# A second MLP in runs of four groups, and two pairs of attention steps of TensorE joined

## The chip, the cores and the metric

The kernel runs on one core of a Trainium2 chip. The metric is the device time of one execution in microseconds (us). The profile comes from one further execution, taken with the hardware profiler on. In what follows PE is TensorE (its matmuls; PEld are its weight loads, which have a row of their own), DVE is VectorE, ACT is ScalarE, POOL is GpSimd and SP is SyncE.

## The reference

```python
for t in range(S):                       # attention with a decaying state, 4 x 8 heads, S = 768, D = 48
    cur = einsum('bhd,bhe->bhde', u * kt, vt)
    y[:, :, t] = einsum('bhd,bhde->bhe', rt, state + cur)
    state = wt * state + einsum('bhd,bhe->bhde', kt, vt)
x = y as (3072 tokens, 384)
x = ((x @ w_a) * (x @ w_b)) @ w_out      # first MLP, 1536 hidden
h = x @ w_in                             # second MLP, 2048 hidden
out = (max(h, 0) + alpha * min(h, 0)) @ w_out2
```

All inputs and the output are float32.

## The kernel before

The sequence is cut into 12 units of the attention, two to a block of 512 tokens; six blocks (`BLOCKS`) go through the first MLP (`mlp1`), and after it six chunks of 512 tokens go through the second (`mlp2`). The attention of the next block is computed beside the first MLP of this one; the second MLP stands alone behind them.

Nothing is issued in the order of the text. Each step is a task (`add`): an engine, a planned duration, a priority (lower goes first), a function that emits the instructions, the names that it reads and writes, and at most one buffer that it takes (`alloc`). `Tasks.run` simulates the engines with the planned durations, picks on each engine the ready task of the lowest priority, and so makes one fixed order for each engine. Buffers of one tag are handed out in the order in which the tasks were added, and a task whose buffer is not free is passed over. On the chip the engines then follow that order, and wait on each other by semaphores; a planned duration alters the order and nothing else.

A product of the MLPs is split in high and low parts (fp32r): `gemm3` is nine matmuls 128*128 on 128x512, three over the depth times (high, high), (low, high), (high, low).

*Second MLP.* A chunk has 16 groups f of 128 hidden channels. `step(f)` computes `hp` (nine matmuls of 512 columns, `gh`, L769 through the helper `mm`) in one of two PSUM banks (tag "h"); DVE makes the leaky rectifier in two instructions (`neg` L923, `pos` L927) in a tile m (tag "a2", three buffers); ACT makes the high part g/h (`hi` L932) and DVE the low part g/l (`lo`, L257) in a tile of tag "g22" (three buffers). `add_out(f)` multiplies g by the output weights in twelve matmuls of 384 columns into four accumulators `acd` (`out2`); three are in banks of tag "acc", the fourth in one of tag "att". The list of tasks puts `add_out(f-1)` behind `step(f)` at the same priority, and which of the two goes first is left to the planner. The weights of both kinds, "i" and "p", are loaded alternately (`w2`) by POOL, and ACT and DVE turn them from float64 into two float32 parts during the last block of the first MLP.

*Attention.* A unit has a tree of decay products on T (DVE), levels `psl` (PE, L567) that read T, then `ktrans`, two steps of four transposes of k from T into two PSUM banks `psk` (PE, L613), each copied by ACT to `kn` (L618); `dstate` (`psd`, L637); `state`; and `yout`, two steps (halves b = 0, 1) of y^T, `psx` (PE, L710), each turned by ACT (L720) and DVE into the first MLP's x. The levels of most units, `psk`, `psd` and `psx` share three banks of tag "att". T has one buffer: the next unit's T is loaded when the last reader of this one is done, and `psk` is among the last.

Of the kernel before, what the change touches and what calls it, by code (L numbers as in the profile page):

```python
# [211 lines left out]
def rwkv_then_moe_kernel(  # L212
# [43 lines left out]
    def tt(out, a, b, op=ALU.mult):  # L256
        nc.vector.tensor_tensor(out=out, in0=a, in1=b, op=op)  # L257
# [4 lines left out]
    def act(n, psum=False):  # L262
        return n / 1200 + (0.05 if psum else 0.093)
# [72 lines left out]
    def unit(u, pr):  # L336
# [34 lines left out]
        def mn(hd, k):  # L371
            return f"M{hd}{k}" if u else f"m{hd}/{k}"

        def zn(cc, hd, k):
            return f"Z{cc}{hd}{k}" if u else f"z{cc}{hd}/{k}"
# [226 lines left out]
            else:  # L602
                nc.scalar.copy(dst, src)

        def ktrans(g, p):
            st = {}
            ps = f"psk{u}_{g}"
# [7 lines left out]
            def cp():  # L615
# [5 lines left out]
            add("ACT", act(448, True), p, cp, r=[ps], w=[f"{kn}/{g}"], alloc=("kn", kn) if g == 0 else None)  # L621

        def dstate(p):

# [67 lines left out]

                add("ACT", act(384, True), p + 6, begin, r=[f"psd{u}_{cc}"], w=s)

        def yout(b, p):


            st = {}
            ps = f"psx{u}_{b}"
            t0 = 256 * (u - us[0]) + 128 * b  # L700
            tag, pool = bank(False)

            def mms():
                st["ps"] = pp.tile([128, 3, 128], F32, tag=tag, name="psx", bufs=3)
                for cc in range(2):
                    for q in range(4):
                        for s, c0, hd, beg, end in (
                                (2 * q, 0, 0, True, True), (2 * q + 1, 32, 1, True, True),
                                (8 + q, 32, 0, True, False), (8 + q, 0, 1, False, True)):
                            nc.tensor.matmul(  # L710
                                out=st["ps"][32 * (s % 4):32 * (s % 4) + 32, s // 4, 64 * cc:64 * cc + 64],
                                lhsT=zt(cc, hd)[:, 4 * b + q, c0:c0 + 32],
                                rhs=mt(hd)[:, cc, 4 * b + q],
                                start=beg, stop=end,
                            )

            def hi():
                if first:
                    X[j] = xp.tile([128, 2, 3, 256 * len(us)], F32R, tag="x", name="x", bufs=2)
                nc.scalar.copy(X[j][:, 0, :, t0:t0 + 128], st["ps"])  # L720

            def lo():
                tt(X[j][:, 1, :, t0:t0 + 128], st["ps"], X[j][:, 0, :, t0:t0 + 128].bitcast(F32), ALU.subtract)

            first = u == us[0] and b == 0
# [3 lines left out]
            add("ACT", act(384, True), p, hi, r=[ps], w=[f"x{j}/{u}{b}h"], alloc=("x", f"x{j}") if first else None)  # L729
            add("DVE", dve(384), p, lo, r=[ps, f"x{j}/{u}{b}h"], w=[f"x{j}/{u}{b}l"])  # L730


        if u:
# [22 lines left out]
        for g in range(2):  # L756
            ktrans(g, pr(0.6))
# [4 lines left out]
        yout(0, pr(0.8))  # L762
        yout(1, pr(0.85))

        return [f"x{j}/{u}{b}{z}" for b in range(2) for z in "hl"]

# [97 lines left out]
    def load_x2(c, p):  # L864
# [20 lines left out]
            add("DVE", dve(512), p, lo, r=[s, f"{xn}/{kt}h"], w=[f"{xn}/{kt}l"])  # L885
        return [f"{xn}/{kt}{z}" for kt in range(3) for z in "hl"]

    def mlp2(c, pr, xn):
        acc = f"acc2_{c}"
        st = {"acc": {}}  # L890

        def out2(f, ks, ts=(0, 1, 2, 3)):
            if f == 0:
                st["acc"][ts[0]] = pp.tile(
                    [128, DM], F32, tag="acc" if ts[0] < 3 else "att", name=f"acd{ts[0]}", bufs=3)
            for i in ks:
                wi, gi = ((0, 0), (1, 0), (0, 1))[i]
                for t in ts:
                    mm(st["acc"][t], st["g", f][:, gi, 128 * t:128 * t + 128], W["p", f][:, wi],
                       f == 0 and i == 0, f == F2 - 1 and i == 2)  # L900

        def add_out(f, p):
            g, wo = f"h{c}_{f}", f"wp{f}"
            accs = [f"{acc}_{t}" for t in range(4)]
            if f in (0, F2 - 1):
                for t in range(4):
                    add("PE", 3 * 0.162, p, lambda t=t: out2(f, (0, 1, 2), (t,)),
                        r=[g + "/h", g + "/l", wo, wo + "/l"], w=[accs[t]],
                        alloc=("psacc" if t < 3 else "psatt", accs[t]) if f == 0 else None)
                return  # L910
            add("PE", 8 * 0.162, p, lambda: out2(f, (0, 1)), r=[g + "/h", wo, wo + "/l"], w=accs)
            add("PE", 4 * 0.162, p, lambda: out2(f, (2,)), r=[g + "/l", wo], w=accs)

        def step(f, p):
            h, m, g = f"ph{c}_{f}", f"m{c}_{f}", f"h{c}_{f}"

            def gh():
                st["h", f] = pp.tile([128, 512], F32, tag="h", name="hp", bufs=2)
                gemm3(st["h", f], W["i", f], X["2", c])

            def neg():
                st["m", f] = P2["p"].tile([128, 512], F32, tag="a2", name="g", bufs=3)
                nc.vector.tensor_scalar(  # L923
                    out=st["m", f], in0=st["h", f], scalar1=0.0, scalar2=al[:, f:f + 1], op0=ALU.min, op1=ALU.mult)

            def pos():
                nc.vector.scalar_tensor_tensor(  # L927
                    out=st["m", f], in0=st["h", f], scalar=0.0, in1=st["m", f], op0=ALU.max, op1=ALU.add)

            def hi():  # L930
                st["g", f] = P2["p"].tile([128, 2, 512], F32R, tag="g22", name="g22", bufs=3)
# [8 lines left out]
            add("ACT", act(512), p - 50, hi, r=[m], w=[g + "/h"], alloc=("g22", g))  # L940
            add("DVE", dve(512), p - 50, lo, r=[m, g + "/h"], w=[g + "/l"])

        for f in range(F2):
            step(f, pr(f))
            if f:
                add_out(f - 1, pr(f))
            elif c:
                st2[c - 1](pr(f))
        def last(p):
            add_out(F2 - 1, p)  # L950
            for t in range(4):
                o = f"o{c}_{t}"

                def cp(t=t):
                    st["o", t] = P2["p"].tile([128, DM], F32, tag="o", name="o", bufs=4)
                    if t % 2:
                        nc.vector.tensor_copy(st["o", t], st["acc"][t])
                    else:
                        nc.scalar.copy(st["o", t], st["acc"][t])

                def wr(t=t):
                    nc.sync.dma_start(out=out[t * S + c * CH:t * S + c * CH + CH, :], in_=st["o", t])

                add("DVE" if t % 2 else "ACT", dve(384) if t % 2 else act(384, True), p - 50, cp, r=[f"{acc}_{t}"], w=[o],
                    alloc=("o", o))
                add("SP", 0.6, p - 50, wr, r=[o], nbytes=128 * 1536)
        st2[c] = last
# [22 lines left out]
    with tc.manual_schedule():  # L990
# [155 lines left out]
```

## Time and profile before

| what | value |
|---|---|
| median of 3 runs | 1027.59 us (1027.45 to 1028.16) |
| profiled execution, its own time | 1034.63 us |
| span of that execution, first to last instruction | 1032.8 us |
| PE busy | 988.8 us (96%) |
| DVE busy | 728.4 us (71%) |
| ACT busy | 434.1 us (42%) |
| granted TensorE clock, mean over the span | 0.986 |

The profiled execution is 7.04 us longer than the median of the runs without a profile. A busy share is a mean over stages that have different limits. Matmuls are pipelined: a row's length holds the tail of its last matmul, so the time that a run of matmuls takes from PE is read from its start to the start of the next row. A row of the timeline merges neighbours of one kind, "x9" being nine matmuls.

### The profile page before, as it was taken

The numbers are of one execution on the slowest core, as the hardware profiler recorded it, in microseconds if no ns is written. First come the engines' busy times: TensorE is split into PE (matmuls) and PEld (weight loads), VectorE is DVE, ScalarE is ACT, GpSimd is POOL, SyncE is SP. The second block draws the span as 40 slices with busy tenths as digits, with TensorE's granted clock in tenths as the row PEclk, the third lists the DMA queues.
The fourth block names the chain that finished last, engine by engine and source line by source line (L and its number), as shares of the span: only waits on it lengthen the run. The fifth ranks groups of instructions, "written<-read, shape, count | busy, mean of one in ns | idle before, by whom it ended". The sixth has DMA issues, their size and how long they took to land.

```text
span 1032.8 us, 22660 instructions
## 1 busy us (share of the span) xinstructions
PE 988.8 (96%) x9616; PEld 850.3 (82%) x9616; DVE 728.4 (71%) x1215; ACT 434.1 (42%) x930; POOL 95.7 (9%) x173
## 2 busy tenths in 40 slices
PE   6869889999999999999999999999999999999998
PEld 5768767778788888878888887989998999999988
DVE  7868897989899898797944667455554554555544
ACT  2475989354353553534347995121221211221111
POOL 3032350100000010001003431000000000000000
PEclk9898999999999999999999999999999999999999
DMA  9483585051441424325115552010010100000000
GB/s 278 107 233 110 143 248 137 33 138 36 130 133 21 125 69 120 88 55 169 20 42 168 169 183 78 1 31 31 1 55 7 31 31 1 1 31 1 31 1 31
DMA packets 75092, 85.70 MB, mean 83 GB/s; under 512 B 55216, under 2 KB 64560, under 8 KB 72368
## 3 DMA queue, kind: packets, MB, share of 16 engines
q1 hardware_dynamic: 67824, 52.81, 19.2%
q0 software_dynamic: 7168, 31.46, 9.5%
q8 instruction: 75, 1.23, 0.5%
q14 instruction: 25, 0.20, 0.1%
HBM read 73.24 MB, written 11.01 MB: 82 GB/s over the span
## 4 chain that ended last, share of the span: by engine, by line
PE 65%; DVE 12%; ACT 10%; DMA 9%; issue 3%; SPq 1%; POOL 0%; ACTq 0%; DVEq 0%; POOLq 0%
PE acd L769 19%; PE hp L769 19%; PE acc L769 7%; PE pa L769 6%; PE pb L769 6%; DVE T L257 3%; DMA T<-in_rkw_t_dram 3%; DVE e L257 2%; PE psl L567 2%; DVE A L486 2%; PE warm L988 2%; ACT ws L301 2%; DMA n<-in_rkw_n_dram 2%; ACT ws L295 2%; PE psx L710 2%
## 5 line engine op out<-in xcount | busy, mean ns | idle before, releaser
L769 PE MATMUL acd<-w,g 128*128 128x384 f32 x1152 | 216.9, 336 | 0.2 <-ACT x L855 0.2
L769 PE MATMUL hp<-x,w 128*128 128x512 f32 x864 | 214.9, 393 | 1.5 <-DVE g L927 1.5
L769 PEld LDWEIGHTS acd<-w,g 128*128 128x128 f32 x1152 | 203.8, 188 | 8.6 <-ACT x L855 0.5
L932 ACT CAST g<-g 128x512 fp32r<-128x512 f32 x96 | 59.8, 623 | 304.1 <-PE acd L769 262.1
L769 PEld LDWEIGHTS hp<-x,w 128*128 128x128 f32 x864 | 161.1, 188 | 31.5 <-DVE g L927 1.9
L769 PE MATMUL acc<-g,w 128*128 128x512 f32 x648 | 173.9, 396 | 0.0
L257 DVE TENSOR_TENSOR g<-g,g 128x512 fp32r<-128x512 f32 x96 | 66.2, 690 | 150.6 <-ACT g L932 150.6
L769 PE MATMUL pb<-x,w 128*128 128x512 f32 x648 | 161.2, 393 | 1.7 <-issue 1.7
L769 PE MATMUL pa<-x,w 128*128 128x512 f32 x648 | 160.7, 392 | 0.0
L769 PEld LDWEIGHTS pb<-x,w 128*128 128x128 f32 x648 | 121.4, 189 | 27.7 <-issue 2.1
L769 PEld LDWEIGHTS pa<-x,w 128*128 128x128 f32 x648 | 120.7, 188 | 26.5 <-ACT w L316 0.5
L769 PEld LDWEIGHTS acc<-g,w 128*128 128x128 f32 x648 | 118.5, 188 | 24.1
L257 DVE TENSOR_TENSOR T<-T 112x1024 f32<-112x1024 f32 (+3 forms) x144 | 116.5, 811 | 21.2 <-DMA T<-in_rkw_t_dram 17.2
L831 ACT CAST g<-a 128x512 fp32r<-128x512 f32 x72 | 44.6, 620 | 132.6 <-DVE a L257 130.0
L923 DVE TENSOR_SCALAR g<-hp,al 128x512 f32<-128x512 f32 x96 | 72.1, 751 | 25.5 <-PE hp L769 23.0
L486 DVE TENSOR_REDUCE A<-e 128x16 f32<-128x768 f32 (+15 forms) x148 | 86.1, 582 | 1.7
L257 DVE TENSOR_TENSOR a<-a,pb 128x512 f32<-128x512 f32 x72 | 49.2, 683 | 28.1 <-PE pb L769 25.7
L927 DVE SCALAR_TENSOR_TENSOR g<-hp,g 128x512 f32<-128x512 f32 x96 | 66.3, 691 | 3.0
L820 ACT COPY a<-pa 128x512 f32<-128x512 f32 x72 | 42.1, 584 | 36.2 <-PE pa L769 35.8
L257 DVE TENSOR_TENSOR g<-a,g 128x512 fp32r<-128x512 f32 x72 | 49.6, 689 | 10.0 <-ACT g L831 10.0
L567 PEld LDWEIGHTS psl<-T 48*16 48x16 f32 (+3 forms) x3072 | 34.3, 99 | 25.8 <-issue 12.2
L567 PE MATMUL psl<-T 48*16 48x16 f32 (+3 forms) x3072 | 38.0, 183 | 15.2 <-DVE T L257 8.4
(68 smaller groups left out, 900.0 us busy)
## 6 DMA issues: line engine op xcount, KB each, us to landing
raw<-in_wt_dram POOLq DMA_DIRECT2D x68, 384.0 KB, 4.1
T<-in_rkw_t_dram SPq DMA_DIRECT2D x12, 1344.0 KB, 9.0
N<-in_rkw_n_dram SPq DMA_DIRECT2D x10, 1152.0 KB, 8.4
x2d<-x POOLq DMA_DIRECT2D x36, 128.0 KB, 2.1
x2r<-x2d SPq DMA_DIRECT2D x36, 128.0 KB, 2.3
out_dram<-o SPq DMA_DIRECT2D x24, 192.0 KB, 1.9
V<-in_v_s_dram SPq DMA_DIRECT2D x11, 384.0 KB, 8.5
Z<-in_v_s_dram SPq DMA_DIRECT2D x44, 96.0 KB, 3.1
```

Of the source, the lines that this page charges most:

```text
L257: nc.vector.tensor_tensor(out=out, in0=a, in1=b, op=op)
L295: nc.scalar.activation(out=c["s"].bitcast(F16).rearrange("p (n b) -> p n b", b=2)[:, :, 1], in_=c["raw"][:, :, 1].bitcast(F32), func=ACTF. ...
L301: nc.scalar.activation(out=c["s"].bitcast(U16).rearrange("p (n b) -> p n b", b=2)[:, :, 0], in_=c["raw"][:, :, 0], func=ACTF.Copy, scale=7 ...
L486: nc.vector.tensor_reduce(out=v[:, :, d:d + (n - 1) * (SUB + 1) + 1:SUB + 1], in_=part(st["e"], 0, n), axis=AX.X, op=ALU.add)
L567: nc.tensor.matmul(out=st["ps"][o0:o0 + ms, cc, q, zc * i:zc * i + zc], lhsT=t[b0:b0 + 48, 1, q0 + q, t0:t0 + ms], rhs=r[b0:b0 + 48, q0 + ...
L710: nc.tensor.matmul(out=st["ps"][32 * (s % 4):32 * (s % 4) + 32, s // 4, 64 * cc:64 * cc + 64], lhsT=zt(cc, hd)[:, 4 * b + q, c0:c0 + 32], ...
L769: nc.tensor.matmul(out=out, lhsT=lhsT, rhs=rhs, start=start, stop=stop)
L820: nc.scalar.copy(c["a", f], c["pa"])
L831: nc.scalar.copy(c["g", f][:, 0], c["a", f])
L923: nc.vector.tensor_scalar(out=st["m", f], in0=st["h", f], scalar1=0.0, scalar2=al[:, f:f + 1], op0=ALU.min, op1=ALU.mult)
L927: nc.vector.scalar_tensor_tensor(out=st["m", f], in0=st["h", f], scalar=0.0, in1=st["m", f], op0=ALU.max, op1=ALU.add)
L932: nc.scalar.copy(st["g", f][:, 0], st["m", f])
```

## The change

Second MLP: the groups go in runs of `RUN` = 4. The products hp of a run use four banks (two of tag "h", two of the attention's three, which a task of no engine, HOST, takes once the attention is over; the third holds the fourth accumulator). Two names force the order: `nxt` makes the output products of a run wait for the next run's hp, `old` makes the hp of a run wait for the output products of the run before the last. PE therefore alternates four groups of hp (36 matmuls) with four groups of output products (48). The g tiles come from five buffers, three of "g22" and two of the first MLP's "g2". The weights' list `w2` has eight "i" first and then four of each kind in turn, as they are used.

Attention: the eight transposes of a unit are one step of PE, which takes two banks. So are both halves of `yout` in units 2 to 11; it is planned at 2 * 2.72 us where the two steps were planned at 1.56 us each. ACT's and DVE's steps behind them stay separate. In units 0 and 1 `yout` keeps its two steps, the second now with priority p + 0.05.

```diff
-        def ktrans(g, p):
+        def ktrans(p):
             def tr():
-                st[g] = pp.tile([128, 4, 112], F32, tag=tag, name="psk", bufs=3)
-                for i in range(4):
-                    nc.tensor.transpose(st[g][:, i], cur["T", u][:, 1, 4 * g + i], idt[0:112, 0:112])
+                for g in range(2):
+                    st[g] = pp.tile([128, 4, 112], F32, tag=tag, name="psk", bufs=3)
+                    for i in range(4):
+                        nc.tensor.transpose(st[g][:, i], cur["T", u][:, 1, 4 * g + i], idt[0:112, 0:112])
...
-            add("PE", 0.4, p, tr, r=[f"{T}/k.{g}", "idt"], w=[ps], alloc=(pool, ps), work=392)
+            add("PE", 0.0, p, lambda: None, w=[f"psk{u}_0"], alloc=(pool, f"psk{u}_0"))
+            add("PE", 0.8, p, tr, r=[f"{T}/k.0", f"{T}/k.1", "idt"], w=[f"psk{u}_0", f"psk{u}_1"],
+                alloc=(pool, f"psk{u}_1"), work=784)
...
-        def yout(b, p):
+        def yout(p):
...
-            add("PE", 1.56, p, mms, w=[ps], alloc=(pool, ps), work=2048,
-                r=[mn(hd, k) for hd in range(2) for k in KM]
-                + [zn(cc, hd, k) for cc in range(2) for hd in range(2) for k in "VS"])
+            if u > 1:
+                add("PE", 0.0, p, lambda: None, w=[f"psx{u}_0"], alloc=(pool, f"psx{u}_0"))
+                add("PE", 2 * 2.72, p, lambda: [mms(0), mms(1)], w=[f"psx{u}_0", f"psx{u}_1"], alloc=(pool, f"psx{u}_1"),
+                    work=4096, r=r)
+            for b in range(2):
+                if not u > 1:
+                    add("PE", 1.56, p + 0.05 * b, lambda b=b: mms(b), w=[ps], alloc=(pool, ps), work=2048, r=r)
...
+    RUN = 4
+
+    def hbank(h):
+        f = int(h.split("_")[1])
+        return h if f % RUN < 2 else f"bank{f % RUN - 2}"
...
+            b = f // RUN * RUN + RUN
+            nxt = [f"ph{c}_{x}" if b < F2 else f"ph{c + 1}_{x - F2}" for x in range(b, b + RUN)] if b < F2 or c + 1 < NCH else []
+            nxt = [hbank(x) for x in nxt]
...
-            add("PE", 8 * 0.162, p, lambda: out2(f, (0, 1)), r=[g + "/h", wo, wo + "/l"], w=accs)
-            add("PE", 4 * 0.162, p, lambda: out2(f, (2,)), r=[g + "/l", wo], w=accs)
+            add("PE", 8 * 0.162, p, lambda: out2(f, (0, 1)), r=[g + "/h", wo, wo + "/l"] + nxt, w=accs)
+            add("PE", 4 * 0.162, p, lambda: out2(f, (2,)), r=[g + "/l", wo], w=accs + [f"run{c}_{f}"])
...
+            b = f // RUN * RUN - 1 - RUN
+            old = [f"run{c}_{b}" if b >= 0 else f"run{c - 1}_{b + F2}"] if b >= 0 or c else []
+            gtag, gpool, gn = ("g22", P2, 3) if f % 5 < 3 else ("g2", {"p": xp}, 2)
...
-            add("PE", 9 * MM, p, gh, r=[f"wi{f}", f"wi{f}/l"] + xn, w=[h], alloc=("psh", h))
+            add("PE", 9 * MM, p, gh, r=[f"wi{f}", f"wi{f}/l"] + xn + old, w=[h], alloc=("psh", h) if f % RUN < 2 else None)
...
         for f in range(F2):
             step(f, pr(f))
-            if f:
-                add_out(f - 1, pr(f))
-            elif c:
-                st2[c - 1](pr(f))
+            if f % RUN == RUN - 1:
+                if f >= RUN:
+                    for x in range(RUN):
+                        add_out(f - 2 * RUN + 1 + x, pr(f - RUN + 1 + x))
+                elif c:
+                    st2[c - 1](pr(0))
...
-        w2 = [("ip"[i], f) for f in range(F2) for i in range(2)]
+        w2 = [("i", f) for f in range(RUN)]
+        for b in range(0, F2, RUN):
+            w2 += [("i", f) for f in range(b + RUN, min(b + 2 * RUN, F2))] + [("p", f) for f in range(b, b + RUN)]
```

## Rows read from the trace of the kernel before

**Rows 1.** Busy time of each engine (instructions) in three stretches; then clock, DMA.

```profile
120.00:160.00 40.00, 35.11 (x628) 27.47 (x628) 35.24 (x64) 34.71 (x75) 15.64 (x20) 0.96 0.66 191
440.00:480.00 40.00, 38.96 (x499) 31.73 (x498) 38.59 (x69) 16.96 (x37) 4.28 (x9) 1.00 0.31 79
650.00:1000.00 350.00, 350.00 (x1760) 317.28 (x1760) 186.87 (x273) 63.26 (x106) 0.00 (x0) 1.00 0.06 19
```

**Rows 2.** The same for instructions on acd alone, then on hp alone.

```profile
650.00:1000.00 350.00, 190.10 (x1008) 178.54 (x1008) 5.49 (x10) 4.82 (x10) 1.00 0.06 19
650.00:1000.00 350.00, 187.03 (x752) 139.84 (x752) 121.05 (x168) 1.00 0.06 19
```

**Rows 3.** Timeline of PE in the second MLP: start, length, what, count.

```profile
754.38 2.24 PE L769 MATMUL hp<-x,w 128*128 128x512 f32 x9
756.46 0.87 PE L769 MATMUL acd<-w,g 128*128 128x384 f32 x4
757.16 2.24 PE L769 MATMUL hp<-x,w 128*128 128x512 f32 x9
759.24 1.57 PE L769 MATMUL acd<-w,g 128*128 128x384 f32 x8
760.66 2.24 PE L769 MATMUL hp<-x,w 128*128 128x512 f32 x9
```

**Rows 4.** Timeline of PE in the first MLP's last block.

```profile
576.28 1.52 PE L769 MATMUL acc<-g,w 128*128 128x512 f32 x6
577.64 2.20 PE L769 MATMUL pa<-x,w 128*128 128x512 f32 x9
579.68 0.84 PE L769 MATMUL acc<-g,w 128*128 128x512 f32 x3
```

**Rows 5.** Timeline of PE, the long runs of hp and of acd.

```profile
635.46 6.33 PE L769 MATMUL hp<-x,w 128*128 128x512 f32 x27
641.63 0.69 PE L769 MATMUL acd<-w,g 128*128 128x384 f32 x3
...
679.10 6.43 PE L769 MATMUL acd<-w,g 128*128 128x384 f32 x36
685.36 2.24 PE L769 MATMUL hp<-x,w 128*128 128x512 f32 x9
```

**Rows 6.** Timeline of PE where the second MLP begins.

```profile
625.42 1.52 PE L769 MATMUL acc<-g,w 128*128 128x512 f32 x6
628.43 2.37 PE L769 MATMUL hp<-x,w 128*128 128x512 f32 x9 [1.49 <-DVE g L927]
...
633.92 0.68 PE L769 MATMUL acd<-w,g 128*128 128x384 f32 x3
634.83 0.80 PE L769 MATMUL acd<-w,g 128*128 128x384 f32 x3 [0.22 <-ACT x L855]
```

**Rows 7.** Timeline of DVE there: the first group's second instruction.

```profile
627.69 0.69 DVE L927 SCALAR_TENSOR_TENSOR g<-hp,g 128x512 f32<-128x512 f32 x1
```

**Rows 8.** Timeline of PE, transposes of two units: in one run, and apart.

```profile
253.46 0.93 PE L613 MATMUL psk<-idt,T 112*128 112x112 f32 x8
254.16 1.63 PE L769 MATMUL acc<-g,w 128*128 128x512 f32 x6
...
293.03 0.55 PE L613 MATMUL psk<-idt,T 112*128 112x112 f32 x4
293.35 1.63 PE L769 MATMUL acc<-g,w 128*128 128x512 f32 x6
294.82 0.55 PE L613 MATMUL psk<-idt,T 112*128 112x112 f32 x4
```

**Rows 9.** Timeline of PE, both halves of yout of one unit.

```profile
317.04 2.70 PE L710 MATMUL psx<-M,Z 128*32 128x64 f32 x128
```

**Rows 10.** Timeline of DVE: the first tree step on a newly loaded T.

```profile
438.97 1.23 DVE L257 TENSOR_TENSOR T<-T 112x1024 f32<-112x1024 f32 x1 [2.66 <-DMA T<-in_rkw_t_dram]
```

**Rows 11.** Waits, whole execution: engine, for whom, us in total, times, longest.

```profile
PE psl L567 <- DVE T L257: 8.4, 7, 2.3
```

More of the change, by code (lines that the diff above doesn't have):

```diff
@@ L618, in cp @@
                 nc.scalar.copy(cur["kn", u][:, 4 * g:4 * g + 4], st[g])
-            add("PE", 0.4, p, tr, r=[f"{T}/k.{g}", "idt"], w=[ps], alloc=(pool, ps), work=392)
-            add("ACT", act(448, True), p, cp, r=[ps], w=[f"{kn}/{g}"], alloc=("kn", kn) if g == 0 else None)
+            add("PE", 0.0, p, lambda: None, w=[f"psk{u}_0"], alloc=(pool, f"psk{u}_0"))
+            add("PE", 0.8, p, tr, r=[f"{T}/k.0", f"{T}/k.1", "idt"], w=[f"psk{u}_0", f"psk{u}_1"],
+                alloc=(pool, f"psk{u}_1"), work=784)
+            for g in range(2):
+                add("ACT", act(448, True), p, lambda g=g: cp(g), r=[f"psk{u}_{g}"], w=[f"{kn}/{g}"],
+                    alloc=("kn", kn) if g == 0 else None)
         def dstate(p):
@@ L715, in mms, with hi, lo @@
                             )
-            def hi():
-                if first:
+            def hi(b, t0):
+                if u == us[0] and b == 0:
                     X[j] = xp.tile([128, 2, 3, 256 * len(us)], F32R, tag="x", name="x", bufs=2)
[L720 to L725, printed above, removed]
-            add("PE", 1.56, p, mms, w=[ps], alloc=(pool, ps), work=2048,
-                r=[mn(hd, k) for hd in range(2) for k in KM]
-                + [zn(cc, hd, k) for cc in range(2) for hd in range(2) for k in "VS"])
-            add("ACT", act(384, True), p, hi, r=[ps], w=[f"x{j}/{u}{b}h"], alloc=("x", f"x{j}") if first else None)
-            add("DVE", dve(384), p, lo, r=[ps, f"x{j}/{u}{b}h"], w=[f"x{j}/{u}{b}l"])
+                nc.scalar.copy(X[j][:, 0, :, t0:t0 + 128], st[b])
+            def lo(b, t0):
+                tt(X[j][:, 1, :, t0:t0 + 128], st[b], X[j][:, 0, :, t0:t0 + 128].bitcast(F32), ALU.subtract)
+            r = ([mn(hd, k) for hd in range(2) for k in KM]
+                 + [zn(cc, hd, k) for cc in range(2) for hd in range(2) for k in "VS"])
+            if u > 1:
[3 more added lines that the diff above has]
+            for b in range(2):
+                t0 = 256 * (u - us[0]) + 128 * b
+                ps = f"psx{u}_{b}"
+                if not u > 1:
+                    add("PE", 1.56, p + 0.05 * b, lambda b=b: mms(b), w=[ps], alloc=(pool, ps), work=2048, r=r)
+                add("ACT", act(384, True), p, lambda b=b, t0=t0: hi(b, t0), r=[ps], w=[f"x{j}/{u}{b}h"],
+                    alloc=("x", f"x{j}") if u == us[0] and b == 0 else None)
+                add("DVE", dve(384), p, lambda b=b, t0=t0: lo(b, t0), r=[ps, f"x{j}/{u}{b}h"], w=[f"x{j}/{u}{b}l"])
         if u:
@@ L755, in unit @@
                 add(e, d, p, lambda hd=hd, b0=b0, bs=bs: rcopy(hd, b0, bs), r=nm(T + "/r", bs), w=[mn(hd, "R")])
-        for g in range(2):
-            ktrans(g, pr(0.6))
+        ktrans(pr(0.6))
         dstate(pr(0.65))
@@ L761, in unit @@
                 state(cc, bs, pr(0.7 + 0.05 * cc))
-        yout(0, pr(0.8))
-        yout(1, pr(0.85))
+        yout(pr(0.8))
         return [f"x{j}/{u}{b}{z}" for b in range(2) for z in "hl"]
@@ L892, in out2 @@
         def out2(f, ks, ts=(0, 1, 2, 3)):
-            if f == 0:
-                st["acc"][ts[0]] = pp.tile(
-                    [128, DM], F32, tag="acc" if ts[0] < 3 else "att", name=f"acd{ts[0]}", bufs=3)
+            if f == 0 and 0 in ks:
+                for t in ts:
+                    st["acc"][t] = P2["b", 2][:, 0:DM] if t == 3 else pp.tile(
+                        [128, DM], F32, tag="acc", name=f"acd{t}", bufs=3)
             for i in ks:
@@ L903, in add_out @@
             g, wo = f"h{c}_{f}", f"wp{f}"
-            accs = [f"{acc}_{t}" for t in range(4)]
+            accs = [f"{acc}_{t}" if t < 3 else "bank2" for t in range(4)]
+            b = f // RUN * RUN + RUN
+            nxt = [f"ph{c}_{x}" if b < F2 else f"ph{c + 1}_{x - F2}" for x in range(b, b + RUN)] if b < F2 or c + 1 < NCH else []
+            nxt = [hbank(x) for x in nxt]
             if f in (0, F2 - 1):
@@ L930, in hi @@
             def hi():
-                st["g", f] = P2["p"].tile([128, 2, 512], F32R, tag="g22", name="g22", bufs=3)
+                st["g", f] = gpool["p"].tile([128, 2, 512], F32R, tag=gtag, name="g22", bufs=gn)
                 nc.scalar.copy(st["g", f][:, 0], st["m", f])
@@ L962, in wr @@
                     nc.sync.dma_start(out=out[t * S + c * CH:t * S + c * CH + CH, :], in_=st["o", t])
-                add("DVE" if t % 2 else "ACT", dve(384) if t % 2 else act(384, True), p - 50, cp, r=[f"{acc}_{t}"], w=[o],
+                add("DVE" if t % 2 else "ACT", dve(384) if t % 2 else act(384, True), p - 50, cp, r=[f"{acc}_{t}" if t < 3 else "bank2"], w=[o],
                     alloc=("o", o))
```

32 lines of the change are left out of this document (19 added, 13 removed).

## Prediction

> **What bounds the kernel now.** I read the stages first. In the second MLP PE is never idle (350.00 us of 350), while DVE works 186.87 us of it and ACT 63.26 [rows 1]: only what PE itself spends counts there, and an engine behind it only if it makes PE wait. Beside the attention PE and DVE are both close to full, PE at 38.96 of 40 us and DVE at 38.59 between 440 and 480, PE at 35.11 between 120 and 160 [rows 1]. The granted clock is 1.00 in the later two stretches, the full level of 2.4 GHz, and 0.96 in the first [rows 1].
>
> A PE that is always busy can still be slow, so I read its timeline by starts. In the first MLP, where every matmul has 512 columns, nine of them take 579.68 - 577.64 = 2.04 us, 226.7 ns each [rows 4]. In the second, nine matmuls hp of the same shape take 756.46 - 754.38 = 2.08 and 759.24 - 757.16 = 2.08 [rows 3]. A run of 27 takes 6.17 us [rows 5]: 18 matmuls more than the run of nine cost 4.09 us, 227 ns each, so after the first nine the pace is that of the first MLP. The output products behave alike: a run of 8 takes 1.42 us [rows 3], one of 36 takes 6.26 [rows 5], so 28 more cost 4.84 us, 172.9 ns each, and the run of 8 holds 1.42 - 8 * 0.173 = 0.04 us on top. So each change of shape on PE costs a little while the pace settles, about 0.04 us at the head of an hp run and 0.02 to 0.04 at the head of an acd run.
>
> The whole stretch says the same without single rows. From 650 to 1000 us there are 752 hp and 1008 acd matmuls [rows 2]. At the settled pace they take 752 * 0.2267 + 1008 * 0.1729 = 170.5 + 174.3 = 344.8 us; 5.2 us are left over. 752 / 9 = 83.6 runs of hp lie in it, each with a run of acd behind it, so a pair of switches costs 5.2 / 83.6 = 0.062 us.
>
> **Second MLP: the runs.** [Rows 3] stand for a pattern: in the whole second MLP PE has 92 runs of hp (90 of nine matmuls, two of 27) and 92 of acd, at 0.062 us a pair 5.7 us. Afterwards `old` and `nxt` leave no choice: 24 runs of 36 and 24 of 48. A long run pays its head once: 6.17 - 27 * 0.2267 = 0.05 us for hp [rows 5] and 0.036 for acd (6.26 - 36 * 0.1729 [rows 5]), so 24 * 0.086 = 2.1 at most, and 24 * 0.062 = 1.5 at least. The saving is 3.6 to 4.2 us. I take 3.9. The bound from below is nothing, if the settling comes with something other than the switch, and from above 5.2 * 96 / 83.6 = 6.0, if the long runs showed none.
>
> The Trainium skill speaks against this term. "TensorE: Matmul & The Clock Gate", section "Back-to-back issue gap", gives the warm gap between matmuls as columns / 2.4 + 2.5 ns, with nothing for the neighbour's shape; an estimate by that page is 215.8 ns for 512 columns and 162.5 for 384, in any order, and runs of four would bring 0. The trace does not agree: 226.7 and 172.9 ns settled, more in the first nine [rows 3 to 5].
>
> **Second MLP: what hides the waits.** A run of hp needs its four banks read by DVE. Between the end of one run of hp and the next lie 48 output products, 48 * 0.173 = 8.3 us; DVE and ACT together spend (186.87 + 63.26) / 83.6 = 3.0 us a group [rows 1], and the first three groups are read while PE computes the next. Eight groups can be alive with five g tiles and three m tiles: the fifth g is made while the run is computed, and each further one when a group of output products, 2.1 us, has given up its tile. The last of four is ready after some 6 to 8 us, and is wanted only 8.3 us later still, after the next run of hp. At the joint of two chunks 15 and 0, 1, 2 all take "g22", so group 2 waits for group 15's products, one run later; nobody needs it for another 8.3 us. I cost this at 0. If that cover were gone, PE would stand up to 2 us at each of 24 joints. The added waits `nxt` and `old` are PE on PE and cost nothing in themselves. Of the loads, POOL issues as many, in another order; the weights of the first eight hp come earlier than now.
>
> **The handover.** Now PE stands twice. The third hp waits for DVE to read the first bank: 628.43 - 625.42 = 3.01 us for six matmuls that need 1.36 [rows 6, 4], 1.65 us lost; DVE reaches `pos` of the first group only at 627.69 [rows 7], 0.7 us before. Then output products wait for accumulators that ACT has not copied out: 634.83 - 633.92 = 0.91 and 635.46 - 634.83 = 0.63 us [rows 6, 5], where three products need 0.52: 0.50 us. Afterwards four hp need no used bank and the output products come behind eight hp, 16.3 us later. At 628.43 two hp are done, and 12 matmuls of the first MLP (2.7 us) are still to come; with two more hp (4.1 us) the fifth hp would start near 628.43 - 1.65 + 6.8 = 633.6, 5 us after `pos` has ended. Both stalls go: -2.15 us. What is late next is the eighth m tile, under the same cover.
>
> **Attention.** Both halves of `yout` stand already as one run of 128 in all 12 units ([rows 9] is one): joined they save 0 in their place. `psk` is one run of eight in five units and two of four in seven. Apart they cost 0.32 + 0.32 us and one more settling (six matmuls behind them take 1.47 us instead of 1.36) against 0.70 together [rows 8, 4]: 0.05 us, times seven 0.35. ACT's copies stay two.
>
> What I can't read is the order. T is loaded anew when `psk` has read it, and DVE waits 2.66 us for it at 438.97 [rows 10]. The second transposes stand 1.79 us behind the first [rows 8]; joined at the first's place they free T up to 1.4 us earlier (1.79 - 0.38), joined at the second's place 0.3 later. All that PE waits for the tree at the levels is 8.4 us, from the start of the kernel on [rows 11]: the gain is 0 to some 5 us. Against that, the planner now believes that `yout` holds PE for 5.44 us instead of 3.12, where a run takes 2.70 [rows 9]. Whatever the plan fills in meanwhile on DVE is 2.3 us less far on the chip, so PE may come to the next level up to 2.3 us too early, in ten units. I take 0 for the order, with -5 and +20 as its ends.
>
> **The sum.** On the profiled execution: 1034.63 - 3.9 - 2.15 - 0.35 = 1028.2 us. The runs without a profile lie 7.04 us lower; I carry that over: 1021.2 us, 0.6% below the median.
>
> **Rivals and chances.** About 0.2% (2 us) is what a measurement of this kernel can tell from no change.
>
> *Forecast*, 0.50: 1021.2, own range 1019 to 1023.5.
>
> *Only the number of columns counts*, in the runs without a profile at least: the settling in the rows comes from something else than the switch, and runs of four bring nothing. The gains at the handover and of the transposes are left: 1027.6 - 2.5 = 1025.1, at the edge of what can be told. Against it stand 84 pairs with 0.062 us each. 0.10, half faster, half the same. It is the rule of the Trainium skill's page "TensorE: Matmul & The Clock Gate" cited above.
>
> *The handover stays*: DVE reads the first bank no earlier, and another step of PE waits for it: 1027.6 - 3.9 - 0.35 = 1023.3. The four free banks speak against it. 0.10.
>
> *The order beside the attention gets worse*: PE arrives at the levels before the tree, because `yout` is planned 2.3 us too long. It decides from 6.4 / 10 = 0.64 us a unit on; at 1 us a unit the time is 1021.2 + 10 = 1031. For it: PE and DVE are both nearly full there [rows 1]. Against it: the first MLP's matmuls run at 226.7 ns where the plan has 215.5, 3.6 us over a block's 324 in the other direction. 0.18: slower 0.12, the same 0.06.
>
> *T comes earlier*: joined transposes take the first's place and the levels wait less: 1021.2 - 3 = 1018. 0.12.
>
> Faster: 0.50 + 0.05 + 0.10 + 0.12 = 0.77; the same 0.05 + 0.06 = 0.11; slower 0.12. The range leaves out most of the worse order and the outer end of the better one: 1016.5 to 1027.5.
>
> **What would show it.** Right: in the second MLP PE has hp in rows of 36 and acd in rows of 48, eight groups per 2 * (8.2 + 8.35) = 33.1 us instead of 8 * 350 / 83.6 = 33.5; no gap of over 1 us on PE between 620 and 645; `psk` only as eight. Wrong: rows of 36 that take over 8.3 us (settling not gone), PE waiting in the second MLP for ACT's or DVE's g, or more idle time of PE before `psl` and `psx` between 100 and 540 than now. The prediction fails if the first MLP ends more than 4 us later than now, or if the second stands at a joint of two runs.

## The result, and the profile after

The changed kernel takes 1037.81 us (median of 6 runs, 1034.29 to 1041.15), the kernel before 1028.69 (6 runs, 1027.45 to 1030.91). The ratio is 1.0086, 95% interval 1.0068 to 1.0103: it is slower. The forecast was 1021.2 us, faster, in a range of 1016.5 to 1027.5. The profiled execution took 1038.25 us, with a span of 1036.5 (before: 1032.8).

I read first the place where the second MLP begins. These are the lines of PE's timeline at the handover after the change; they answer to [rows 6]:

```profile
630.79 2.20 PE L778 MATMUL hp<-x,w 128*128 128x512 f32 x9
...
635.55 1.52 PE L778 MATMUL acc<-g,w 128*128 128x512 f32 x6
636.91 2.20 PE L778 MATMUL hb<-x,w 128*128 128x512 f32 x9
```

Six matmuls take 636.91 - 635.55 = 1.36 us, where [rows 6] has 3.01: PE no longer stands there. (hb are the attention's banks.) The first hp is at 630.79. The kernel before had its first at 620.66, some 10 us earlier; from there to the end of the span it is 405.67 us instead of 412.18, 6.5 us less. The second MLP gained what was forecast, and the part ahead of it lost 10.1 us in this pair of profiles.

The start of the execution hides a part of the loss: the first product of the first MLP, pa, is at 79.77, and was at 83.01 before. From there to the first hp, before and after (PE, PEld, DVE, ACT, POOL; then the granted clock):

```profile
83.01:620.66 537.65, 523.10 (x6166) 427.29 (x6165) 446.34 (x782) 309.44 (x687) 71.51 (x134) 1.00 0.39 111
79.77:630.79 551.02, 529.91 (x6166) 430.28 (x6165) 450.99 (x787) 311.26 (x694) 65.84 (x137) 0.99 0.40 110
```

The stretch is 13.4 us longer. For as many matmuls PE is idle 21.1 us instead of 14.6, and busy 6.8 us longer: one half of the loss is waits, and the other half slower matmuls. The mean granted clock, 0.988 instead of 0.997 to three digits, accounts for about 5 us of the 6.8 (an estimate: the missing share of the clock times the length of the stretch, 6.8 us instead of 1.7).

The second MLP itself, PE's timeline of one run of four groups and the head of the next run:

```profile
676.76 4.28 PE L778 MATMUL hp<-x,w 128*128 128x512 f32 x18
680.89 4.24 PE L778 MATMUL hb<-x,w 128*128 128x512 f32 x18
684.97 0.69 PE L778 MATMUL acd<-w,g 128*128 128x384 f32 x3
...
693.31 4.28 PE L778 MATMUL hp<-x,w 128*128 128x512 f32 x18
```

36 matmuls of hp take 684.97 - 676.76 = 8.21 us, and four whole groups 693.31 - 676.76 = 16.55 us. Before, four took 4 * 350 / 83.6 = 16.75 [rows 1, 2].

Beside the attention the stretches say where to look (PE, PEld, DVE, ACT, POOL; then the granted clock; they answer to [rows 1]):

```profile
120.00:160.00 40.00, 34.20 (x616) 27.22 (x615) 35.49 (x65) 37.61 (x79) 13.90 (x24) 0.91 0.75 214
440.00:480.00 40.00, 37.15 (x511) 29.94 (x510) 33.85 (x62) 12.87 (x31) 2.13 (x4) 0.96 0.29 72
650.00:1000.00 350.00, 350.00 (x1777) 319.41 (x1777) 191.18 (x280) 64.43 (x108) 1.07 (x2) 1.00 0.06 20
```

Between 440 and 480 PE works 37.15 us of 40 instead of 38.96, and DVE 33.85 instead of 38.59: both are less busy, so both wait. The granted clock is 0.96 there, where it was 1.00; between 120 and 160 it is 0.91, where it was 0.96. The waits name a pair (engine, for whom, us in total, times, longest):

```profile
PEld pb L778 <- DVE a L257: 10.0, 9, 3.3
...
PE pb L778 <- DVE a L257: 6.5, 5, 2.9
```

The kernel before has no such row. The largest of these waits, in PE's timeline:

```profile
446.99 2.70 PE L713 MATMUL psx<-M,Z 128*32 128x64 f32 x128
449.62 2.35 PE L778 MATMUL pb<-x,w 128*128 128x512 f32 x9
451.80 1.53 PE L778 MATMUL acc<-g,w 128*128 128x512 f32 x6
...
455.21 0.84 PE L778 MATMUL acc<-g,w 128*128 128x512 f32 x3
458.90 3.55 PE L778 MATMUL pb<-x,w 128*128 128x512 f32 x9 [2.85 <-DVE a L257]
462.24 1.99 PE L778 MATMUL acc<-g,w 128*128 128x512 f32 x6
464.07 2.23 PE L778 MATMUL pa<-x,w 128*128 128x512 f32 x9
```

and what DVE did in the meantime (its whole timeline from the load of T to the product that PE waits for):

```profile
449.11 1.23 DVE L257 TENSOR_TENSOR T<-T 112x1024 f32<-112x1024 f32 x1 [2.49 <-DMA T<-in_rkw_t_dram]
450.26 0.85 DVE L486 TENSOR_REDUCE A<-e 128x14 f32<-128x672 f32 x1
451.02 0.54 DVE L257 TENSOR_TENSOR St<-St,psd 112x384 f32<-112x384 f32 x1
451.48 0.80 DVE L257 TENSOR_TENSOR N<-N 128x624 f32<-128x624 f32 x1
452.20 0.69 DVE L257 TENSOR_TENSOR T<-T 112x512 f32<-112x512 f32 x1
452.80 0.80 DVE L257 TENSOR_TENSOR e<-N 128x624 f32<-128x624 f32 x1
453.52 1.22 DVE L257 TENSOR_TENSOR T<-T 112x1024 f32<-112x1024 f32 x1
454.66 0.80 DVE L486 TENSOR_REDUCE A<-e 128x13 f32<-128x624 f32 x1
455.37 0.61 DVE L257 TENSOR_TENSOR T<-T 112x256 f32<-112x256 f32 x1
455.90 0.75 DVE L257 TENSOR_TENSOR e<-kn,N 128x576 f32<-128x576 f32 x1
456.57 1.21 DVE L257 TENSOR_TENSOR T<-T 112x1024 f32<-112x1024 f32 x1
457.70 0.55 DVE L257 TENSOR_TENSOR x<-psx,x 128x384 fp32r<-128x384 f32 x1
458.17 0.68 DVE L257 TENSOR_TENSOR a<-a,pb 128x512 f32<-128x512 f32 x1
```

These two orders do not fit together in time. The y^T step of this unit ran on PE from 446.99 and gave way to pb at 449.62, 2.63 us later; it was planned at 5.44. DVE first waits 2.49 us for T, then works off eleven instructions of the attention, and only then subtracts for x and multiplies a by pb. On PE the instruction behind that pb starts at 451.80; the product that empties its bank comes at 458.17, and the next pb has to wait for the bank. Then nine matmuls take 462.24 - 458.90 = 3.34 us instead of 2.04, and six 1.83 instead of 1.36: the clock has dropped (last section).

The longest single wait of PE in the stretch has no name in that view. It stands before a level; PE's timeline, and the step of DVE that ends ahead of it:

```profile
139.85 1.63 PE L567 MATMUL psl<-T 48*24 48x16 f32 x128 [3.33 <-issue]
141.42 2.93 PE L778 MATMUL acc<-g,w 128*128 128x512 f32 x6
144.14 2.94 PE L778 MATMUL pb<-x,w 128*128 128x512 f32 x9
...
138.53 1.22 DVE L257 TENSOR_TENSOR T<-T 112x1024 f32<-112x1024 f32 x1
```

The level reads T, and starts 0.10 us after DVE's tree step has ended at 139.75. In the kernel before PE stands 0.56 us before the same level (at 143.47), again until 0.10 us after that tree step, so I read the wait as one for the tree, though the view says "issue". Six matmuls behind it take 144.14 - 141.42 = 2.72 us instead of 1.36.

### The profile page after: what moved, and what is told of

Read it like the earlier page. It is cut to its first block, busy times and chain, and to the rows that moved or that the text cites. A ratio compares the mean times of both kernels' runs of the same rounds, so it can differ in the third digit from the quotient of the medians.

```text
span 1036.5 us, 22638 instructions
## 1 busy us (share of the span) xinstructions
PE 989.9 (96%) x9612; PEld 851.6 (82%) x9612; DVE 730.1 (70%) x1215; ACT 432.3 (42%) x930; POOL 87.5 (8%) x173
## 4 chain that ended last, share of the span: by engine, by line
PE 70%; DVE 15%; ACT 6%; DMA 5%; issue 3%; SPq 0%; DVEq 0%; ACTq 0%
PE acd L778 14%; PE hb L778 14%; PE hp L778 10%; PE pb L778 8%; PE acc L778 8%; PE pa L778 8%; DVE T L257 4%; DVE e L257 3%; DVE A L486 3%; DMA T<-in_rkw_t_dram 3%; PE warm L1026 2%; PE psl L567 2%; DMA n<-in_rkw_n_dram 2%; PE psx L713 1%; DVE N L257 1%
## 5 line engine op out<-in xcount | busy, mean ns | idle before, releaser
L778 PE MATMUL acd<-w,g 128*128 128x384 f32 x864 | 192.7, 335 | 0.0
L778 PE MATMUL acc<-g,w 128*128 128x512 f32 x648 | 176.0, 400 | 0.5 <-issue 0.5
L778 PE MATMUL pb<-x,w 128*128 128x512 f32 x648 | 163.7, 398 | 6.6 <-DVE a L257 6.5
L778 PE MATMUL pa<-x,w 128*128 128x512 f32 x648 | 162.1, 395 | 1.9 <-ACT a L829 1.9
L778 PEld LDWEIGHTS acd<-w,g 128*128 128x128 f32 x864 | 154.2, 188 | 1.8
L778 PEld LDWEIGHTS pb<-x,w 128*128 128x128 f32 x648 | 121.6, 190 | 35.7 <-DVE a L257 10.0
L778 PEld LDWEIGHTS pa<-x,w 128*128 128x128 f32 x648 | 122.0, 190 | 29.9 <-ACT a L829 3.6
L778 PEld LDWEIGHTS acc<-g,w 128*128 128x128 f32 x648 | 120.1, 190 | 25.6 <-issue 0.9
L257 DVE TENSOR_TENSOR T<-T 112x1024 f32<-112x1024 f32 (+3 forms) x144 | 116.1, 808 | 14.3 <-DMA T<-in_rkw_t_dram 9.3
L257 DVE TENSOR_TENSOR g<-g,g 128x512 fp32r<-128x512 f32 x96 | 66.2, 690 | 81.2 <-ACT g L960 80.7
L778 PE MATMUL hp<-x,w 128*128 128x512 f32 x432 | 102.9, 391 | 0.0
L778 PE MATMUL hb<-x,w 128*128 128x512 f32 x432 | 102.0, 389 | 0.0
L778 PEld LDWEIGHTS hb<-x,w 128*128 128x128 f32 x432 | 81.1, 188 | 16.8
L778 PEld LDWEIGHTS hp<-x,w 128*128 128x128 f32 x432 | 80.8, 188 | 16.0
L778 PE MATMUL hb<-w,g 128*128 128x384 f32 x288 | 92.7, 335 | 0.0
L951 DVE TENSOR_SCALAR g<-hp,al 128x512 f32<-128x512 f32 x48 | 36.0, 751 | 63.0 <-PE hp L778 63.0
L257 DVE TENSOR_TENSOR a<-a,pb 128x512 f32<-128x512 f32 x72 | 49.1, 683 | 37.6 <-PE pb L778 33.5
L257 DVE TENSOR_TENSOR g<-a,g 128x512 fp32r<-128x512 f32 x72 | 49.5, 688 | 18.6 <-ACT g L840 18.5
```

What stands on the lines that cost most here:

```text
L778: nc.tensor.matmul(out=out, lhsT=lhsT, rhs=rhs, start=start, stop=stop)
L951: nc.vector.tensor_scalar(out=st["m", f], in0=st["h", f], scalar1=0.0, scalar2=al[:, f:f + 1], op0=ALU.min, op1=ALU.mult)
```

## The experiments

Ratios are to the kernel before in the same series, with their 95% intervals; the medians of the kernel before were 1030.14, 1028.90, 1027.73 and 1029.80 us in the four series, so ratios are compared, not times. Counts of matmuls between psk and psx are counted in PE's order as it was written out.

**One part each.** The first has the second MLP of the changed kernel and `ktrans` and `yout` of the one before; the second the reverse.

> The second MLP's part alone, with the attention of the kernel before. If the whole loss lies beside the attention (every theory of a wrong order there): the first hp starts where it did before (near 620.7 us), the second MLP takes 405.7 us instead of 412.1 as in the changed kernel's profile, and the time is 6.4 us under the kernel before, near 1022. If the runs of four cost something elsewhere, for example by other names that alter the plan beside the first MLP: not under 1026.

Measured: 1024.94 us, ratio 0.9951 (0.9928 to 0.9974). In its profile the first hp starts at 615.02, and from there to the end of the span of 1020.70 it is 405.7 us, as in the changed kernel. (Ahead of it this kernel has the order of the kernel before, whose first hp is at 620.66. From the first pa to the first hp it takes 534.1 us, where the kernel before has 537.7: profiles of one order differ by some 3 us there, so the ratios are the better figure.)

> The attention's part alone, with the second MLP of the kernel before. If the two parts add up: the last product of the first MLP 10 us later than before, as in the changed kernel, and a time near 1028.5 + 10 = 1038.5 or a little above the changed kernel's, since the gain of the second MLP is missing: 1038 to 1046. If the loss needs both parts: near 1028.

Measured: 1043.17 us, ratio 1.0138 (1.0109 to 1.0167). From the first pa to the first hp its profile has 551.4 us, as the changed kernel's (551.0). The two parts add up: 0.9951 * 1.0138 = 1.0088, the changed kernel has 1.0086. The whole loss, some 14 us, is the attention's part.

**Its planned time.** In three kernels one number of the changed kernel is altered, and no instruction:

```diff
-                add("PE", 2 * 2.72, p, lambda: [mms(0), mms(1)], ...
+                add("PE", 2 * 1.56, p, lambda: [mms(0), mms(1)], ...   # 2 * 2.11 and 2 * 1.32 in the others
```

> The changed kernel with one number altered: the joined y^T step is planned at 3.12 us (2 * 1.56) instead of 5.44. Theory of the planned duration (DVE's order is filled with attention work for a PE time that does not exist, and the first MLP's banks then wait for DVE): the waits of pb for DVE go, the first MLP ends about 10 us earlier, 1022 to 1025. Rival, the joined step itself (two banks at once, both halves wait for the last input): unchanged, 1036 to 1040. Rival, the joined transposes: unchanged too.

> The changed kernel with the joined y^T step planned at 4.22 us, halfway between 3.12 (1022.8 us) and 5.44 (1037.8). The instructions are the same, the order differs: between psk and psx of units 6 to 10 stand 81, 51, 45, 42, 45 matmuls of the first MLP, against 81, 63, 81, 63, 81 at 3.12 and 30, 27, 30, 27, 30 at 5.44. Theory (the planned time moves the y^T step ahead, in front of the next unit's T, and the first MLP's products then wait behind attention work on DVE): in between, 1026 to 1033. Rival (any altered order falls somewhere, by chance): no relation, anywhere from 1021 to 1040.

> The changed kernel with the joined y^T step planned at 2.64 us, what it takes on the chip. Between psk and psx stand 78 to 81 matmuls of the first MLP in units 4 to 10. Theory of the planned duration: like 3.12 or a little better, 1020 to 1024. Rival by chance: anywhere from 1021 to 1040.

| planned, us | ratio | interval | median, us |
|---|---|---|---|
| 2.64 | 0.9952 | 0.9935 to 0.9970 | 1024.40 |
| 3.12 | 0.9938 | 0.9917 to 0.9960 | 1022.78 |
| 4.22 | 1.0017 | 0.9999 to 1.0035 | 1030.62 |
| 5.44 (the change) | 1.0086 | 1.0068 to 1.0103 | 1037.81 |

A number that only the planner sees is worth 15 us, and the time rises with it step by step above 3.12 (at 2.64 and 3.12 the intervals overlap). The kernel planned at 3.12 is faster than the kernel before, joined steps and all, and no slower than the second MLP's part alone (0.9951; the intervals overlap). In its profile only a weight load waits for DVE's product before pb, once, for 0.2 us. The wait before the level at 139.85 goes with the number too: it is 1.58 us at 2.64, 1.01 at 3.12, 2.19 at 4.22 and 3.33 at 5.44.

**Apart, and planned too long.** The attention of the kernel before, second MLP in runs of four, and

```diff
-            add("PE", 1.56, p, mms, w=[ps], ...
+            add("PE", 1.56 if u < 2 else 2.72, p, mms, w=[ps], ...
```

> The second MLP in runs of four with the attention of the kernel before (transposes and y^T in two steps each), each y^T step planned at 2.72 us instead of 1.56 in units 2 to 11. Between psk and psx stand 24 to 27 matmuls of the first MLP in units 7 to 11. Theory of the planned duration: nothing needs to be joined for the loss, 1033 to 1040. Rival (the loss needs joined steps): like the second MLP's part alone, 1022 to 1027.

Measured: 1034.02 us, ratio 1.0052 (1.0030 to 1.0074), against 0.9951 with 1.56: 1% for the number, with nothing joined. The wait of pb for DVE is in its profile too ("PEld pb L769 <- DVE a L257: 5.9, 6, 2.5"), and so is that before the level, 3.01 us.

**Place or time.** The changed kernel, its y^T step later by priority, so that it stands behind the next unit's T again:

```diff
-                add("PE", 2 * 2.72, p, lambda: [mms(0), mms(1)], ...
+                add("PE", 2 * 2.72, p + 18, lambda: [mms(0), mms(1)], ...   # and the step that takes the first bank
```

> The changed kernel, planned at 5.44 us as it is, with the y^T step's priority 18 later in units 2 to 11: 81 to 84 matmuls of the first MLP stand between psk and psx in units 4 to 11, as in the good orders. If the place of the step is what costs (it comes before the next T has landed): 1021 to 1026. If the planned time itself costs wherever the step stands (DVE's order is filled for 2.8 us of PE time that the chip does not need, in each of ten units): still over 1031.

Measured: 1033.36 us, ratio 1.0042 (1.0026 to 1.0058), over 1031 as the second expectation has it. Against 1.0086 the place is worth 0.44%, 4.5 us; against 0.9938, where nearly the same place (63 to 81 matmuls in units 6 to 10, here 81 to 84) goes with 3.12 us, the planned time is worth 1% by itself. The product is no longer what PE waits for most; ACT's copy of pa is ("PEld pa L778 <- ACT a L829: 10.0, 8, 2.1"). The wait before the level stays, 3.37 us.

**The plan made true.** The y^T step issues its matmuls twice in units 2 to 11, and so should take 2 * 2.63 = 5.27 us:

```diff
-                add("PE", 2 * 2.72, p, lambda: [mms(0), mms(1)], ...
+                add("PE", 2 * 2.72, p, lambda: [mms(0, 2), mms(1, 2)], ...   # all matmuls of a half twice, same start and stop
```

> The changed kernel, order and plan as they are (5.44 us), but the joined y^T step of units 2 to 11 issues its matmuls twice into the same banks (the second time gives the same sums), so that it takes 5.27 us on the chip, nearly what is planned. That is 10 * 2.63 = 26.3 us more work for PE. If PE loses time in the changed kernel because it is early for an order made for 5.44 us, the added work fills its waits: the waits of pb for DVE go, and the time rises by 15 to 20 us only, to 1053 to 1058. If the loss has nothing to do with PE being early, the whole of it comes on top: 1062 to 1066.

> The same doubling in the kernel planned at 3.12 us (1022.8 us), as a measure of what 26.3 us of PE work cost where the order was made for a short step: if PE has little to wait for there, 22 to 26 us more, 1045 to 1049. If both kernels rise by the same amount, the theory that the added work fills waits falls.

Measured: 1050.77 us, ratio 1.0223 (1.0185 to 1.0261), and 1046.83 us, ratio 1.0188 (1.0145 to 1.0231). The same matmuls, 26.3 us of work as expected, cost 1.37% (14 us) in the changed kernel, even less than expected, and 2.50% (26 us) in the one planned at 3.12. The rises differ by 1.1%, give or take some 0.6 (an estimate from the four intervals). By the profiles the ten steps take more than expected, as there are stalls in them: 64.7 us instead of 29.8, and 59.9 instead of 29.1. PE's timeline at the place of the wait above, in the changed kernel with the work doubled:

```profile
453.31 3.58 PE L714 MATMUL psx<-M,Z 128*32 128x64 f32 x182
457.79 1.70 PE L714 MATMUL psx<-M,Z 128*32 128x64 f32 x74 [0.89 <-issue]
459.41 2.33 PE L779 MATMUL pb<-x,w 128*128 128x512 f32 x9
...
464.98 0.84 PE L779 MATMUL acc<-g,w 128*128 128x512 f32 x3
465.66 2.20 PE L779 MATMUL pb<-x,w 128*128 128x512 f32 x9
```

The second pb follows acc at once (465.66 - 464.98 = 0.68 us for three), where it waited 2.85 us, and no wait of pb for DVE is left among its waits; before the level PE does not stand at all. Some 12 us of PE's added work (26.3 - 14) went into time that was lost already: PE was early for its order.

**The transposes.** With y^T in two steps of 1.56 us again (transposes joined), and with the transposes in two steps again (y^T as changed):

```diff
-        ktrans(pr(0.6))
+        for g in range(2):
+            ktrans(g, pr(0.6))
```

> The changed kernel with y^T in two steps of 1.56 us as before; transposes joined, second MLP in runs of four. If the y^T step is the cause, by its plan or by its join: 1021 to 1025. If the joined transposes are the cause: 1034 to 1040.

> The changed kernel with the transposes of k in two steps as before; y^T joined and planned at 5.44 us, second MLP in runs of four. If the planned time alone makes the loss: 1033 to 1040. If the joined transposes make a part of it (with y^T apart at 1.56 us a kernel with joined transposes took 1031.1 and one with them apart 1024.9, in one series): 1028 to 1032.

Measured: y^T apart 1031.09 us, ratio 1.0018 (0.9995 to 1.0041); transposes apart 1032.39 us, ratio 1.0047 (1.0020 to 1.0073). Neither fits an expectation well: the first lies between its two, the second just above the upper bound of one and below the other. Joined transposes are 0.7% worse than transposes apart with y^T apart at 1.56 (0.9951), 0.4% worse with y^T joined at 5.44 (the intervals overlap a little), and with y^T joined at 3.12 the kernel is at 0.9938, no worse than with everything apart; a kernel with y^T joined at 3.12 and the transposes apart was not run. So no fixed price of the joined transposes is shown; they alter the order as well.

**The instruction stream.** In the profiles of the changed kernel and of the one with y^T apart PE stands in the midst of a level. PE's timeline of the changed kernel:

```profile
325.75 1.16 PE L567 MATMUL psl<-T 48*16 48x16 f32 x121
328.97 0.23 PE L567 MATMUL psl<-T 48*16 48x16 f32 x7 [2.07 <-issue]
329.13 0.97 PE L778 MATMUL acc<-g,w 128*128 128x512 f32 x3
329.94 3.81 PE L778 MATMUL pa<-x,w 128*128 128x512 f32 x9
333.58 2.22 PE L778 MATMUL pb<-x,w 128*128 128x512 f32 x9
```

After 121 of 128 matmuls nothing comes for 2.07 us, and nothing releases it but "issue"; then nine matmuls take 3.64 us. Three kernels have more warming matmuls at the start, where PE waits anyway, and are otherwise unchanged:

```diff
             warm["ps"] = pp.tile([128, 512], F32, tag="h", name="warm", bufs=2)
+            for _ in range(16):
+                nc.tensor.matmul(out=warm["ps"][:, 0:128], lhsT=idt, rhs=idt, start=True, stop=True)
```

> The changed kernel with 16 more warming matmuls (32 in the trace's count) at the very start, where PE waits for the first level anyway; order and plan are unchanged. If the stall of 2.2 us in the seventh unit's level (326.7 us) belongs to a place in PE's instruction stream, it comes 32 matmuls earlier in the level (after some 89 of 128 instead of 121) or goes; if it is gone with the half clock behind it, up to 3.8 us less. If it is a wait for data, it stays after 121 of 128.

> The same with 32 more warming matmuls (64 in the count): the stall after some 57 of 128, or gone. The warming at the start may now take 1 to 3 us of the first level's time. By the rival (data), it stays after 121 of 128.

> The kernel with y^T apart at 1.56 us and joined transposes (1031.1), with 16 more warming matmuls at the start. By the instruction stream: its stall of 2.4 us at 322.2 moves by 32 matmuls or goes, and the time falls by 0 to 4 us. By data: no change.

Measured: 1034.85 us, ratio 1.0058 (1.0034 to 1.0083); 1034.21 us, 1.0039 (1.0011 to 1.0066); 1029.18 us, 0.9996 (0.9974 to 1.0019). The level in the profile with 16 more:

```profile
325.83 1.22 PE L567 MATMUL psl<-T 48*16 48x16 f32 x128
326.98 0.97 PE L778 MATMUL acc<-g,w 128*128 128x512 f32 x3
327.78 2.23 PE L778 MATMUL pa<-x,w 128*128 128x512 f32 x9
```

It runs through, and so do the levels at this place in the other two. The stall belongs to the place in PE's stream of instructions. Two things in the traces support that. In five profiles of four different orders (the changed kernel, its attention's part alone, those planned at 4.22 and 2.64, and the one with y^T apart) a stall stands behind the same number of matmuls on PE, 4675. And a packet of the queue that the page of the profile calls "instruction" (q8: 75 packets of 16 KB in the execution, one for about 128 matmuls) starts at 326.60, 2.37 us before PE goes on; in the other four profiles it is 2.38 or 2.39 us.

All three are 0.2 to 0.5% below their originals, but the intervals of two of the pairs overlap, and in each of the three another such stall came up elsewhere: 2.72 us at 141.00, 1.27 at 310.90 and 2.16 at 414.17. The kernel before has one as well, 1.67 us at 147.69. So moving the count trades stalls, and what this one cost in the changed kernel, up to 2.1 + 1.6 us by its profile, is not measured better. The wait before the level at 139.85 is none of these: with the count moved it stands before the same step (3.13 and 4.22 us).

**Runs of two.** The second MLP's part alone with `RUN = 2`.

> The second MLP's part alone, attention as before, but in runs of two groups (RUN = 2): 48 pairs of switches instead of 24 or 92. If each pair costs 0.062 to 0.086 us, four groups take 16.55 us + one more pair = 16.61 to 16.64 in the profile (16.74 before the change, 16.55 in runs of four). With two banks for hp the wait of the third hp at the handover, 1.65 us, may come back; the time lies 1 to 4 us above the second MLP's part in runs of four (1024.9). If the settling is not by the switch: 16.55 or 16.74 and no step between.

Measured: 1031.02 us, ratio 1.0039 (1.0020 to 1.0057). Its second MLP, heads of runs of hp on PE (two runs, and the head of the third):

```profile
713.45 4.28 PE L769 MATMUL hp<-x,w 128*128 128x512 f32 x18
...
730.06 4.28 PE L769 MATMUL hp<-x,w 128*128 128x512 f32 x18
```

Four groups take 730.06 - 713.45 = 16.61 us, as expected: 16.55, 16.61 and 16.75 us with one pair of switches in four groups, with two, and with 92 / 24 = 3.8. The time is worse than expected, in part because two waits came back at the handover, one of them longer:

```profile
622.77 2.35 PE L769 MATMUL hp<-x,w 128*128 128x512 f32 x9 [1.40 <-DVE g L946]
...
633.93 0.79 PE L769 MATMUL acd<-w,g 128*128 128x384 f32 x3 [2.79 <-ACT x L855]
```

With two groups the first output products come before ACT has copied the accumulators out, and behind that wait the granted clock is 0.67 from 633.9 to 639.0. So at the handover it is the run of four that takes the waits away, by its length or by the four banks that go with it; the two were not told apart.

## Why the prediction was wrong

**The runs of four** were right. Settling pays by the pair of switches, 0.06 us, at three run lengths. The Trainium skill's formula in "TensorE: Matmul & The Clock Gate", section "Back-to-back issue gap", which the page gives for the gap of one matmul by itself and which knows the number of columns alone, does not describe the three: with the same matmuls it gives one time for four groups, where the rows have 16.55, 16.61 and 16.75 us.

**The handover** was right: both stalls are gone. Forecast for runs and handover together were 3.9 + 2.15 = 6.05 us; the profiles have 412.18 - 405.67 = 6.51, and the part alone has 0.49% (5 us, interval 2.7 to 7.4). No joint of two runs showed a wait of PE: it is busy 350.00 of 350 us.

**The step that failed** is in the attention's part: "I take 0 for the order, with -5 and +20 as its ends." It was +14 us (1.0138). The rival named the mechanism, "the planner now believes that `yout` holds PE for 5.44 us instead of 3.12", and the runs show it as the cause: the number alone, altered, takes the loss away and in between lies in between; the number alone, put on steps that are not joined, makes over two thirds of it; real work in the planned length fills PE's waits. That DVE's order makes up the whole of the 14 us isn't shown: the waits for its product and before the level, with the slow clock behind them, are most of what the profile names, and a stall of the instruction stream comes on top. What was wrong was the weight. I set against it that the plan is 3.6 us a block too short for the first MLP's matmuls. That shortfall is spread over 324 matmuls, about 11 ns each; the 2.8 us lie in one place, and DVE's order is filled there. A sum over a block says nothing of an order.

**The place of the wait** was right once and wrong for the most part. I expected PE too early at the levels, in each of ten units. One level is late as the rival has it, by 3.33 us instead of 0.56, and latest where the planned time is longest; but from 100 to 540 us PE is idle 10.4 us before psl and psx together, and was 10.1 before. It is the first MLP that waits: pb's bank for DVE's product, 6.5 us on PE's own row. The loss is 1.4 us a unit (14 / 10) rather than the 1 us that the rival took. The sign that I had named for being wrong came true, the first MLP's end more than 4 us later. The longer plan also moved the y^T step itself: between psk and psx stand 27 to 30 matmuls of the first MLP in units 6 to 10, and 75 to 90 before. It now came ahead of the next T, at a time when DVE had nothing to do (2.49 us) and then everything at once. I had costed "joined they save 0 in their place" and not asked whether the place would stay. The runs give about 4.5 us for the place and 10 for the planned time where the place is the old one, in one pair of orders.

**The transposes'** 0.05 us a unit could not be told from the change of order they bring. Why joined transposes cost 0.4 to 0.7% in two orders stays open. Stalls of the instruction stream may account for a part: with its stall moved, and another come up, the kernel with y^T apart is at 0.9996, where the one with transposes apart has 0.9951.

**T earlier**: it did not pay. DVE's first tree step at the place shown still waits, 2.49 us instead of 2.66 [rows 10]. Over the whole execution DVE waits 9.3 us for T where it waited 17.2; but what PE waits for the tree at the levels, 8.4 us before [rows 11], is 6.7 by name and the 3.33 of 139.85 besides.

## What to carry to other kernels

In a kernel whose order comes from a planner, a planned duration is part of the program: where it exceeds the real one on a busy engine, the other engines' queues are filled for time that does not exist, and the busy engine is stopped at the first short buffer, or the first result, that it needs from them. Here that cost 15 us of 1023. Compare every planned duration with the row in the trace before looking at what the step does. A change of shape on PE costs little each time (0.06 us a pair here), so it is worth gathering only where PE is the sole bound, and there the run of four with its four banks also took away the waits at the stage's start.

## What the hardware showed that I had not expected

The clock fell behind PE's longest waits, in a stage that is otherwise full. Busy times and granted clock of the changed kernel around two of the stalls shown above:

```profile
455.00:459.00 4.00, 1.15 (x6) 0.65 (x4) 4.00 (x7) 0.12 (x1) 0.00 (x0) 1.00 0.00 0
459.00:463.00 4.00, 4.00 (x11) 3.22 (x12) 4.00 (x7) 0.98 (x2) 0.00 (x0) 0.59 0.02 4
...
326.00:329.00 3.00, 0.93 (x114) 0.82 (x99) 2.96 (x8) 0.62 (x1) 0.00 (x0) 1.00 0.03 8
329.00:333.00 4.00, 4.00 (x18) 3.18 (x19) 3.90 (x11) 1.45 (x4) 0.00 (x0) 0.62 0.01 4
```

PE was busy 1.15 of 4 us, then 0.93 of 3, at full clock; in the 4 us behind, busy throughout, the granted clock is 0.59 and 0.62, most of it at the lower level of 1.2 GHz. The 15 matmuls from 458.90 to 464.07 take 5.17 us instead of 3.40. So a stall of 2.85 us cost 4.6, and one of 2.07 us 3.7 (2.07 and 3.64 - 2.04 for nine matmuls). Behind the wait before the level the clock is 0.50 from 139.8 to 143.0. It is not so behind every wait: after PE stood 1.67 us before pa at 293.54, it is 1.00 up to 297.5.

A run of small matmuls can stop at a place in the instruction stream, by all signs for want of instructions: 2.07 us behind 4675 matmuls, gone from there when the count was moved by 32 or 64 matmuls with order and data the same, and 2.37 us behind the start of a packet of the instruction queue. In the rows it is known by "issue" in the midst of a group. "Issue" ahead of a group can be something else: the wait of 3.33 us ended with a step of DVE.
